# Three mixtures in one launch: remainders, sums and row transposes moved in the instruction order of an attention and two expert layers

## The chip, the cores and the metric

The kernel runs on one core of a Trainium2 chip, as one launch. The metric is the device time of a run in microseconds (us). All work is in float32, or in pairs of rounded float32 values (below).

## The reference

The computation has three parts. The first is an attention with random features. With 4 batches, 8 heads, 576 rows and 64 columns, and 128 features `omega`, it is, cut to what matters:

```python
def phi(x):                       # x scaled by D ** -0.25
    h = x @ omega.T - sum(x * x) / 2
    return exp(h - max(h)) / sqrt(m)
kv = k_p.T @ v;  z = sum(k_p)
attn = (q_p @ kv) / (q_p @ z + 1e-06)
```

The second is a dense mixture over 2304 rows of 512 columns, with 8 experts of 1024 hidden columns. `P` is a table of 2304 x 8 weights, made of the gate's logits by 8 rounds of row and column normalization:

```python
for e in range(8):
    out += P[:, e:e+1] * (relu(x @ w1[e]) @ w2[e])
```

The third is a sparse mixture on the result. A row whose product with `w_skip` is not over 0 is passed through. Each other row goes to the one expert with its largest logit, and has `gate * (relu(x @ w1[e]) @ w2[e])` added.

## The kernel before

**Pairs.** A float32 value is split into a copy rounded for TensorE (`hi`, made on ScalarE) and the *remainder* (`lo`, value minus copy, a subtraction that mostly runs on VectorE). A product is then three matmuls: hi by hi, hi by lo, lo by hi. Each engine runs its instructions in the order in which the code issues them. Buffers are waited for: an instruction that writes a buffer waits until the last reader of its earlier content is done.

**Attention.** 36 units of work (9 of k, 9 of q, and the same for the second half) run through a pipeline, one unit entering per `step`. `stage_a` transposes a unit into a PSUM bank `pt` (L426), copies it (`xh`, L429) and makes its remainder (`xl`, L431). `stage_b` projects it into `pa` (L456), takes the maximum and makes the bias `nb` (L459 to L461). `stage_x` is the exponentials (L469). For k, `stage_ck` adds up `kvp` (L489). For q, `stage_cq` transposes the result in two groups into PSUM banks `pb` (L524) and copies them (`qpt`, L525), `stage_dq` forms the quotient (L549 to L564), and `stage_eq` transposes that for the next layer into a `pb` (L589). `pt` and all `pb` share two PSUM banks, tag "b" of the pool `ps_b`. Steps 12, 21 and 30, where k turns to q or q to k, are `turn`; those and steps 11, 20 and 29 are `quiet`. In quiet steps the code puts the subtraction for `xl` into a list `rest` and issues it behind `stage_b`.

**Dense mixture.** It goes in three passes over 768 rows each. A pass has 32 steps, 8 experts by 4. Pass 0 is written in `first` and `second`. Passes 1 and 2 are written in `fast`, which works out each product of 2 x 2 blocks from seven products of sums and differences instead of eight. Step n has seven *first products* for itself (L305, six matmuls each) and, between them, seven *second products* for step n - 1 (`prod2`, six matmuls each, L1133). From the first products come seven combinations `ct[n, 0]` to `ct[n, 6]`. VectorE adds (L1239, L1265, L1279), ScalarE applies relu, GpSimd weighs by `P` (L1199) and combines (L1203). Each combination is split by `hi_a` (L1208, ScalarE) and `lo_a` (L1211, VectorE). The order of the second products, with the combination that each reads first, is

```python
SEC = ((0, 0, (0, 0)), (1, 1, 0), (3, 3, (1, 1)), (2, 6, 2), (4, 4, (0, 1)), (6, 2, 1), (5, 5, (1, 0)))
```

So the fifth reads combination 4, the sixth combination 6 and the seventh combination 5. The second and the sixth add up in PSUM banks of their own through the whole pass. The others share banks 2 and 3, and VectorE adds each of them to a sum in SBUF at once (L1144), which frees the banks for the next of them. The order of a step on TensorE is: first products 0 and 1, second 0, first 2, second 1, first 3, second 2, first 4, second 3, first 5, second 4, first 6, seconds 5 and 6.

**Sums of a pass.** `fin_steps` combines the seven sums into the four quarters of the result (L1150 is its `add`). Behind pass 1 its parts are spread over the next steps; behind pass 2 they stand in the code that follows the loop.

**The end.** Behind the last step, its second products alternate with the first products of the sparse mixture: two slots of 128 rows of the largest expert, whose rows are known early, through `split_a` (L1319 and L1321) and `products_a` (L1345). Then `route` makes the logits of the last two groups of rows from the sums (L826), picks experts and counts them on VectorE (L837 to L854), has the counts added up on TensorE (L869 to L879), and GpSimd writes the rows' numbers into a table. `rows_of_sums` transposes the sums into rows (L804, copies L805) and sends them to memory. The remaining slots follow one after the other, their experts read from that table.

Of the kernel before, what the change touches and what calls it, by code (L numbers as in the profile page):

```python
# [9 lines left out]
F32 = mybir.dt.float32  # L10
# [4 lines left out]
OP = mybir.AluOpType  # L15
# [6 lines left out]
def attn_moe_moe_kernel(  # L22
# [15 lines left out]
    nc = tc.nc  # L38
# [5 lines left out]
    P = 128  # L44
    KD = DM // P
# [371 lines left out]
            )  # L417
        loaded[nm, half, i] = t

    st, rest = {}, []  # L420

    def stage_a(nm, half, i):
        x = loaded[nm, half, i].rearrange("p h d -> p (h d)")
        pt = ps_b.tile([P, 512], F32, tag="b", name="pt")
        for c in range(KD):
            nc.tensor.transpose(pt[:, c * P : (c + 1) * P], x[:, c * P : (c + 1) * P], ident)  # L426
        xh = t_p.tile([P, KD, P], F32R, tag="xh", name="xh")
        xl = t_p.tile([P, KD, P], F32R, tag="xl", name="xl")
        nc.scalar.copy(xh, pt)  # L429
        rest.append(  # L430
            lambda: nc.vector.tensor_tensor(xl, pt.rearrange("p (c t) -> p c t", c=KD), xh.bitcast(F32), OP.subtract)  # L431
        )
        if not quiet:
            rest.pop()()
        x2 = t_p.tile([P, H, D], F32, tag="x2", name="x2")
        nc.gpsimd.tensor_tensor(x2.rearrange("p h d -> p (h d)"), x, x, OP.mult)
        st[nm, half, i] = [xh, xl, x2]
# [216 lines left out]
    for step in range(nj + 7):  # L654
# [51 lines left out]
        if step == 1:  # L706
            heat(2)
        run(1, stage_b)
        if rest:
            rest.pop()()  # L710
        if turn:
            run(3, stage_ck, "k")
            run(1, put_v)
# [432 lines left out]
    def fin_steps(p, ys=None):  # L1146

        quarter = lambda g, f: sums(p)[:, 2 * f : 2 * f + 2, g * GW : (g + 1) * GW]
        e1, e6, e7, e5 = quarter(0, 0), quarter(0, 1), quarter(1, 0), quarter(1, 1)
        add = lambda o, x: nc.vector.tensor_tensor(o, x, o, OP.add)  # L1150

        def add_y(o, k):
            if ys:
                add(o, ys[k])
            elif k == 2:
                add(o, e4)
            else:
                for h in range(2):
                    add(o[:, h], yb[BANKS[k][h]][:, :GW])

        def end():
            for t in range(2 * GT):
                done(p, t)

        return {
            "6+1": lambda: add(e6, e1),
            "7+6": lambda: add(e7, e6),
            "6+5": lambda: add(e6, e5),
            "5+7": lambda: add(e5, e7),
            "1+0": lambda: add_y(e1, 0),  # L1170
            "6+3": lambda: add_y(e6, 1),
            "7+4": lambda: add_y(e7, 2),
            "end": end,
        }

    def fin(p, n):
# [29 lines left out]
    def hi_a(n, a):  # L1206
        ha[n, a] = h_tiles(n)
        nc.scalar.copy(ha[n, a][0], ct[n, a])  # L1208

    def lo_a(n, a):  # L1210
        nc.vector.tensor_tensor(ha[n, a][1], ct[n, a], ha[n, a][0].bitcast(F32), OP.subtract)  # L1211

    def split_a2(n, a):
        hi_a(n, a)
        lo_a(n, a)

    def fast(n, x_next):
# [3 lines left out]
        def sec(j):  # L1221
            if pf:
                prod2(n - 1, j)
            elif j < 2 * GT:
                second(n - 1, j)
# [13 lines left out]
        nc.vector.tensor_tensor(c1, pz[:, :GW], c1, OP.add)  # L1239
        if pf:  # L1240
            lo_a(n - 1, 1)
            lo_a(n - 1, 4)
        weigh(n, 0, 0)
        if pf:
            split_a2(n - 1, 6)
            hi_a(n - 1, 5)
        x_next(2)
        pump(None, "pool")
        sec(0)
        product(py, 4, 4, n, False)  # L1250
        c2 = ct[n, 1] = c_tile(1)
        nc.scalar.copy(c2, py[:, :GW])
# [34 lines left out]
        x_next(8)  # L1287
        sec(5)
        sec(6)

    def drain():
        while side:
# [28 lines left out]
            eng.tensor_tensor(lo, t, hi.bitcast(F32), OP.subtract)  # L1321
        return hi, lo

    def split_a(s, r, c, part=None):

        if not 0 < s < NE:
            eng = nc.vector
            if r:
                tag = ("raw1", "raw1", "raw2", "wsum")[c]
                if part == 1:  # L1330
                    t = wa[c, r]
                else:
                    t = w1s_p.tile([P, 2, DM], F32R, tag=tag, name="sw1", bufs=2 + (c < 2))
                    t = t[:, 0], t[:, 1]
                wa[c, r] = split(zc[c], *t, eng, part)
            else:
                t = wa[c, r] if part == 1 else [xg_p.tile([P, DM], F32R, tag=f"x{x}{c}", name="sx" + x) for x in "hl"]
                wa[c, r] = split(ebuf[1][:, c], *t, eng, part)
# [46 lines left out]
    for n, (p, e, i) in enumerate(steps):  # L1385
# [57 lines left out]
        if p:  # L1443
            if p > 1 and e == 0 and i == 0:
                fin(p - 1, n)
            fast(n, x_next)
            if i == 0 and n + KI < ns_:
                load_pw(*steps[n + KI][:2])
            fetch_w2(n + 1)
            if n == ns_ - 2 * KI:  # L1450
                e_1 = reg_at(reg0, 0, [ET.Pool], E - 1)
                w_0 = rows_of(w1b, e_1), rows_of(w2b, e_1)
                nc.gpsimd.dma_start(ebuf[1][:, :KD], w_0[0][:, :, : FF // 2])
                plan[ns_ - 1, 2] = [lambda: first_w(0, 1)]
                for pos, c, part in ((3, 0, 0), (4, 0, 1), (4, 1, 0), (5, 1, 1)):
                    plan.setdefault((ns_ - 1, pos), []).append(lambda c=c, part=part: split_a(0, 0, c, part))
                plan[ns_ - 2, 8] = [first_x]
            if n == ns_ - 1:
                first_w(2, 3)
            continue  # L1460
# [38 lines left out]
    hbs += [xg_p.tile([P, FF // 2], F32, tag=tag, name="hb") for tag in ("xh6", "xl6")]  # L1499
    do = fin_steps(NP - 1)  # L1500
    split_a2(end_, 1)
    lo_a(end_, 4)
    p1 = m_bank()
    products_a(0, p1, range(0, 2))
    split_a(0, 0, 2)
    prod2(end_, 0)
    split_a2(end_, 6)
    prod2(end_, 1)
    split_a(0, 0, 3)
    products_a(0, p1, range(2, 3))  # L1510
    prod2(end_, 2)
    split_a2(end_, 5)
    do["6+1"]()
    prod2(end_, 3)
    for c in range(KD):
        split_a(0, 1, c, 0)
    products_a(0, p1, range(3, 4))
    nc.scalar.activation(out=hbs[0], in_=p1, func=AF.Relu)
    for k in (4, 5):
        xhs.append(xg_p.tile([P, KD, P], F32R, tag=f"xh{k}", name="xhs"))  # L1520
        xls.append(xg_p.tile([P, KD, P], F32R, tag=f"xl{k}", name="xls"))
    xsplit(1)
    do["1+0"]()
    prod2(end_, 4)
    do["7+6"]()
    p1 = m_bank()
    products_a(0, p1, range(0, 2), 1)
    prod2(end_, 5)
    do["6+5"]()
    prod2(end_, 6)  # L1530
    products_a(0, p1, range(2, 4), 1)
    do["6+3"]()
    do["5+7"]()
    do["7+4"]()
    mst.close()
# [116 lines left out]
    def go(r, n=1):  # L1652
        for _ in range(n):
            next(r)

    go(ra, GT - 1)
    for c in range(2):
        split_a(0, 1, c, 1)
    hsplit(0, 0, 1)
    go(ra)  # L1660
    go(rb, GT)
    go(ra)
    go(ta, GT)
    write_out()
    split_b(0, 0, 1, 2, 3, part=0)
    for c in range(2, KD):
        split_a(0, 1, c, 1)
    go(rb)
    p1 = ps_p.tile([P, 512], F32, tag="p1", name="p1")
    products_a(1, p1, range(0, 2))  # L1670
    go(tb, GT)
    writes += last
    write_out()
    yst.close()
    ps_1 = ctx.enter_context(tc.tile_pool(name="ps_1", bufs=2, space=PSUM))
    pys = [ps_1.tile([P, 512], F32, tag=f"py{i}", name=f"py{i}", bufs=1) for i in range(2)]
    split_b(0, 0, 1, part=1)
    products_a(1, p1, range(2, 4))
    relu(1, p1)
    hsplit(1, 0, 0)  # L1680
    hsplit(0, 1, 0)
    p1 = ps_p.tile([P, 512], F32, tag="p1", name="p1")
    products_a(1, p1, range(0, 1), 1)
    hsplit(1, 0, 1)
    split_b(0, 2, 3, part=1)
    split_b(0, 4, 5, 6, 7, part=0)
# [105 lines left out]
```

## Time and profile before

| | |
|---|---|
| runs | 1778.37, 1778.49, 1782.36 us; median 1778.49 |
| profiled execution | 1779.85 us, span 1778.3 us |
| granted clock of TensorE, mean | 0.996 |
| TensorE matmul busy | 1750.8 us of the span |
| VectorE busy | 1391.4 us |
| ScalarE, GpSimd busy | 857.4 and 846.2 us |

Engines are PE (TensorE matmul), PEld (its weight loads), DVE (VectorE), ACT (ScalarE), POOL (GpSimd) and SP. L305 is line 305 of the kernel before. Times are counted from the span's start. The matmuls' ends are modelled, and one begins before the last has ended; so the distance between two starts tells more than a matmul's own time, and an idle time shown for PE is short of what a wait cost.

### The profile page before, as it was taken

How to read it: one execution, taken by the hardware profiler on the slowest of the kernel's cores; microseconds unless marked ns; L12 is line 12 of the kernel's file. 1: busy time of each engine (PE TensorE's matmuls, PEld its weight loads, DVE VectorE, ACT ScalarE, POOL GpSimd, SP SyncE). 2: the span in 40 equal slices, each digit the busy share in tenths (PEclk: the TensorE clock that was granted, in tenths of full speed). 3: DMA queues.
4: the chain of work that ended last, by engine and by line, in shares of the span. 5: the costliest groups of instructions: out<-in, count | busy, mean ns of one | idle time of the engine just before them, and what ended most of it. 6: DMA issues, size and time to landing. Idle time of an engine off the chain costs nothing. (4 is left out here: it accounts for less than half of the span.)

```text
span 1778.3 us, 29140 instructions
## 1 busy us (share of the span) xinstructions
PE 1750.8 (98%) x10181; PEld 1664.9 (94%) x10181; DVE 1391.4 (78%) x2546; ACT 857.4 (48%) x1870; POOL 846.2 (48%) x857
## 2 busy tenths in 40 slices
PE   9999999999999999999999999999999999999998
PEld 9989988888888888999999999999999999999876
DVE  7868477767776777787888888888887888787887
ACT  6858444444444444434444444454443444344476
POOL 5243044436644443554555555545554555455442
PEclk9999999999999999999999999999999999999999
DMA  8241378879998888987876768787778778787271
GB/s 212 75 141 38 123 285 282 293 285 348 331 315 308 298 323 331 343 259 254 284 251 230 287 248 312 269 315 252 257 242 278 246 263 262 270 284 248 99 258 51
DMA packets 224336, 446.81 MB, mean 251 GB/s; under 512 B 25880, under 2 KB 120184, under 8 KB 224176
## 3 DMA queue, kind: packets, MB, share of 16 engines
q1 hardware_dynamic: 220592, 437.14, 71.2%
q0 software_dynamic: 3312, 7.61, 1.2%
q8 instruction: 83, 1.36, 0.3%
q14 instruction: 77, 0.63, 0.1%
q10 hardware_dynamic: 272, 0.07, 0.0%
HBM read 323.47 MB, written 134.83 MB: 258 GB/s over the span
## 5 line engine op out<-in xcount | busy, mean ns | idle before, releaser
L305 PE MATMUL m<-xh,w1h 128*128 128x384 f32 x1330 | 446.0, 335 | 0.3 <-DVE x L1309 0.2
L305 PE MATMUL m<-xl,w1h 128*128 128x384 f32 x1330 | 445.6, 335 | 0.0
L305 PE MATMUL m<-xh,w1l 128*128 128x384 f32 x1330 | 444.6, 334 | 0.0
L1199 POOL TENSOR_TENSOR c<-c,pw 128x384 f32<-128x384 f32 x192 | 214.8, 1119 | 448.7 <-ACT c L1198 447.3
L305 PEld LDWEIGHTS m<-xh,w1h 128*128 128x128 f32 x1330 | 249.7, 188 | 9.8 <-DVE rc L776 0.9
L305 PEld LDWEIGHTS m<-xl,w1h 128*128 128x128 f32 x1330 | 249.7, 188 | 8.6
L1144 DVE TENSOR_TENSOR eb<-y,eb 128x384 f32<-128x384 f32 x496 | 251.8, 544 | 0.3
L305 PEld LDWEIGHTS m<-xh,w1l 128*128 128x128 f32 x1330 | 249.7, 188 | 0.0
L1133 PE MATMUL y<-hh,wb 128*128 128x384 f32 x768 | 196.9, 337 | 0.2 <-DVE e L1144 0.2
L1211 DVE TENSOR_TENSOR hl<-c,hh 128x384 fp32r<-128x384 f32 x192 | 150.1, 782 | 47.2 <-ACT hh L1208 47.2
L1211 DVE TENSOR_TENSOR hl<-s,hh 128x384 fp32r<-128x384 f32 x256 | 185.9, 739 | 1.4
L1198 ACT ACTIVATE c<-c 128x384 f32<-128x384 f32 x192 | 101.1, 527 | 175.3 <-DVE c L1279 82.3
L1133 PE MATMUL y<-hh,w2h 128*128 128x384 f32 x512 | 173.4, 339 | 4.3 <-DVE eb L1144 4.3
L1133 PE MATMUL y<-hl,w2h 128*128 128x384 f32 x512 | 171.4, 335 | 0.0
L1133 PE MATMUL y<-hh,w2l 128*128 128x384 f32 x512 | 171.3, 335 | 0.0
L1208 ACT CAST hh<-c 128x384 fp32r<-128x384 f32 x192 | 98.7, 514 | 121.6 <-POOL c L1199 119.1
L1037 PE MATMUL y<-w2h,hl 128*128 128x512 f32 x384 | 152.4, 397 | 0.0
L1037 PE MATMUL y<-w2l,hh 128*128 128x512 f32 x384 | 151.7, 395 | 0.0
L1037 PE MATMUL y<-w2h,hh 128*128 128x512 f32 x384 | 149.5, 389 | 0.0
L1208 ACT CAST hh<-s 128x384 fp32r<-128x384 f32 x256 | 123.1, 504 | 33.5 <-POOL s L1203 33.4
L1133 PEld LDWEIGHTS y<-hh,wb 128*128 128x128 f32 x768 | 137.6, 188 | 0.7 <-DVE e L1144 0.5
L1203 POOL TENSOR_TENSOR s<-c,c 128x384 f32<-128x384 f32 x128 | 130.5, 1020 | 5.7 <-DVE c L1271 0.9
(347 smaller groups left out, 3527.5 us busy)
## 6 DMA issues: line engine op xcount, KB each, us to landing
wb<-w2c SPq DMA_DIRECT2D x128, 384.0 KB
w1h<-w1c SPq DMA_DIRECT2D x64, 640.0 KB
w1l<-w1c SPq DMA_DIRECT2D x64, 640.0 KB
w2h<-w2c SPq DMA_DIRECT2D x64, 512.0 KB
w2l<-w2c SPq DMA_DIRECT2D x64, 512.0 KB
w2c<-eb SPq DMA_DIRECT2D x58, 512.0 KB
w1c<-w1h SPq DMA_DIRECT2D x32, 896.0 KB
w1c<-w1l SPq DMA_DIRECT2D x32, 896.0 KB
```

Source lines behind the costliest of these rows:

```text
L305: nc.tensor.matmul(ps[:, :GW], x[:, a, c, :], y[:, c, :], start=first and m == 0, stop=m == 3 * KC - 1, skip_group_check=True,)
L1037: nc.tensor.matmul(ys[t], a[:, ts], b[:, f], start=i == 0 and f == 0 and m == 0, stop=i == KI - 1 and f == 1 and m == 2,)
L1133: nc.tensor.matmul(o, x[:, h * P : (h + 1) * P], y, start=m == 0 and (own or e == i == 0), stop=m == 2 and (own or e == E - 1 and i == KI ...
L1144: nc.vector.tensor_tensor(dst[:, h], o, dst[:, h], OP.add)
L1198: nc.scalar.activation(out=t, in_=t, func=AF.Relu)
L1199: nc.gpsimd.tensor_tensor(t, t, pw[steps[n][:2]][:, g], OP.mult)
L1203: nc.gpsimd.tensor_tensor(t, ct[n, x], ct[n, y], op)
L1208: nc.scalar.copy(ha[n, a][0], ct[n, a])
L1211: nc.vector.tensor_tensor(ha[n, a][1], ct[n, a], ha[n, a][0].bitcast(F32), OP.subtract)
```

## The change

- In the attention, the list `rest` goes. The subtraction for `xl` is issued in `stage_a` right behind the copy in all steps, the quiet ones too.
- In `fast`, the remainder of combination 4 is issued at the end of its own step, behind the last second product, instead of behind the first two first products of the next step. The remainder of combination 6 is issued behind the first second product, and so behind its sums of L1144, instead of ahead of them. The rounded copies stay where they were.
- In the last step, the remainders for the first two blocks of the sparse mixture's weights go to GpSimd, and the order of copies and remainders is changed.
- Behind the last step, the sums are formed in another order: "6+1" and the new "4+6" run on GpSimd; "5+6", "6=5+3" take the place of "7+6", "6+5" and "6+3". Remainders and copies there change places with products.
- In the routing, one remainder (`hsplit(0, 0, 1)`) moves behind the first group's counts, and the row transposes of both groups alternate with single blocks of `products_a` instead of standing together. A transposition of the hidden block changes places with a product.

```diff
-    st, rest = {}, []
+    st = {}
...
-        rest.append(
-            lambda: nc.vector.tensor_tensor(xl, pt.rearrange("p (c t) -> p c t", c=KD), xh.bitcast(F32), OP.subtract)
-        )
-        if not quiet:
-            rest.pop()()
+        nc.vector.tensor_tensor(xl, pt.rearrange("p (c t) -> p c t", c=KD), xh.bitcast(F32), OP.subtract)
...
         run(1, stage_b)
-        if rest:
-            rest.pop()()
...
-        add = lambda o, x: nc.vector.tensor_tensor(o, x, o, OP.add)
+        add = lambda o, x, eng=nc.vector: eng.tensor_tensor(o, x, o, OP.add)
...
-            "6+1": lambda: add(e6, e1),
+            "6+1": lambda: add(e6, e1, nc.vector if ys else nc.gpsimd),
...
+            "5+6": lambda: add(e5, e6),
+            "4+6": lambda: add(e4, e6, nc.gpsimd),
+            "6=5+3": lambda: [
+                nc.vector.tensor_tensor(e6[:, h], yb[BANKS[1][h]][:, :GW], e5[:, h], OP.add) for h in range(2)
+            ],
...
             lo_a(n - 1, 1)
-            lo_a(n - 1, 4)
         weigh(n, 0, 0)
         if pf:
-            split_a2(n - 1, 6)
+            hi_a(n - 1, 6)
             hi_a(n - 1, 5)
         x_next(2)
         pump(None, "pool")
         sec(0)
+        if pf:
+            lo_a(n - 1, 6)
...
         sec(5)
         sec(6)
+        lo_a(n, 4)
...
-                for pos, c, part in ((3, 0, 0), (4, 0, 1), (4, 1, 0), (5, 1, 1)):
-                    plan.setdefault((ns_ - 1, pos), []).append(lambda c=c, part=part: split_a(0, 0, c, part))
+                for pos, c, part in ((3, 0, 0), (4, 1, 0), (4, 0, 1), (4, 1, 1)):
+                    plan.setdefault((ns_ - 1, pos), []).append(
+                        lambda c=c, part=part: split_a(0, 0, c, part, nc.gpsimd)
+                    )
...
     split_a2(end_, 1)
-    lo_a(end_, 4)
...
-    split_a2(end_, 6)
+    hi_a(end_, 6)
     prod2(end_, 1)
-    split_a(0, 0, 3)
+    split_a(0, 0, 3, 0)
+    do["6+1"]()
     products_a(0, p1, range(2, 3))
+    split_a(0, 0, 3, 1)
     prod2(end_, 2)
-    split_a2(end_, 5)
-    do["6+1"]()
+    hi_a(end_, 5)
+    lo_a(end_, 6)
+    products_a(0, p1, range(3, 4))
     prod2(end_, 3)
-    for c in range(KD):
-        split_a(0, 1, c, 0)
-    products_a(0, p1, range(3, 4))
...
+    do["1+0"]()
     xsplit(1)
-    do["1+0"]()
     prod2(end_, 4)
-    do["7+6"]()
+    lo_a(end_, 5)
+    for c in range(KD):
+        split_a(0, 1, c, 0)
+    do["4+6"]()
     p1 = m_bank()
     products_a(0, p1, range(0, 2), 1)
     prod2(end_, 5)
-    do["6+5"]()
+    do["5+6"]()
     prod2(end_, 6)
     products_a(0, p1, range(2, 4), 1)
-    do["6+3"]()
+    do["6=5+3"]()
     do["5+7"]()
     do["7+4"]()
...
+    go(ra)
     hsplit(0, 0, 1)
-    go(ra)
     go(rb, GT)
     go(ra)
-    go(ta, GT)
+    p1 = ps_p.tile([P, 512], F32, tag="p1", name="p1")
+    for c in range(2):
+        go(ta)
+        products_a(1, p1, range(c, c + 1))
+    go(ta)
     write_out()
...
     go(rb)
-    p1 = ps_p.tile([P, 512], F32, tag="p1", name="p1")
-    products_a(1, p1, range(0, 2))
-    go(tb, GT)
+    for c in range(2, KD):
+        go(tb)
+        products_a(1, p1, range(c, c + 1))
+    go(tb)
...
-    products_a(1, p1, range(2, 4))
     relu(1, p1)
     hsplit(1, 0, 0)
-    hsplit(0, 1, 0)
     p1 = ps_p.tile([P, 512], F32, tag="p1", name="p1")
     products_a(1, p1, range(0, 1), 1)
+    hsplit(0, 1, 0)
```

## Rows read from the trace of the kernel before

**Rows 1.** Busy time, granted clock (PEclk), DMA share and GB/s of five stretches (us).

```profile
97.00:103.00 6.00, 4.53 (x26) 4.53 (x27) 2.06 (x8) 2.88 (x10) 0.00 (x0) 0.72 0.00 1
143.00:148.00 5.00, 4.04 (x20) 3.83 (x20) 1.98 (x4) 1.97 (x6) 1.04 (x1) 0.66 0.18 52
...
210.00:640.00 430.00, 429.88 (x2143) 383.98 (x2142) 312.40 (x488) 201.27 (x390) 205.64 (x220) 1.00 0.85 302
640.00:1640.00 1000.00, 996.26 (x5719) 981.25 (x5718) 813.57 (x1485) 428.62 (x900) 516.79 (x486) 1.00 0.79 274
1640.00:1700.00 60.00, 56.54 (x332) 50.06 (x331) 49.83 (x125) 27.16 (x54) 24.97 (x30) 1.00 0.39 136
```

**Rows 2.** TensorE's waits, 40 to 160 us: total, times, longest.

```profile
PE pb L524 <- DVE xl L431: 4.2, 3, 2.0
PE pb L589 <- DVE xl L431: 2.3, 2, 1.9
PE pt L426 <- ACT qpt L525: 1.4, 2, 0.7
PE pb L524 <- ACT qpt L525: 1.3, 1, 1.3
```

**Rows 3.** TensorE's waits, 640 to 1640 us.

```profile
PE y L1133 <- DVE eb L1144: 3.7, 18, 0.2
```

**Rows 4.** TensorE's waits, 1640 to 1700 us.

```profile
PE m L1345 <- DVE sxl L1321: 0.7, 1, 0.7
PE y L1133 <- DVE eb L1144: 0.7, 1, 0.7
PE m L804 <- ACT rows L805: 0.7, 1, 0.7
...
PE y L1133 <- DVE e L1144: 0.2, 1, 0.2
```

**Rows 5.** TensorE in order of time, pass 1: start, length, idle before.

```profile
947.21 0.34 PE L305 MATMUL m<-xh,w1l 128*128 128x384 f32 x1
947.77 0.44 PE L1133 MATMUL y<-hh,w2h 128*128 128x384 f32 x1 [0.22 <-DVE eb L1144]
948.05 0.34 PE L1133 MATMUL y<-hh,w2l 128*128 128x384 f32 x1
```

**Rows 6.** VectorE in order of time, step 20 of the attention.

```profile
97.74 0.68 DVE L431 TENSOR_TENSOR xl<-pt,xh 128x512 fp32r<-128x512 f32 x1
```

**Rows 7.** TensorE in order of time, step 21 of the attention.

```profile
98.47 0.66 PE L589 MATMUL pb<-ident,x 128*128 128x128 f32 x4 [1.88 <-DVE xl L431]
```

**Rows 8.** VectorE in order of time, the step of rows 5 and its end.

```profile
944.43 1.06 DVE L1211 TENSOR_TENSOR hl<-c,hh 128x384 fp32r<-128x384 f32 x1
945.41 1.84 DVE L1211 TENSOR_TENSOR hl<-s,hh 128x384 fp32r<-128x384 f32 x2
947.17 1.01 DVE L1144 TENSOR_TENSOR eb<-y,eb 128x384 f32<-128x384 f32 x2
948.11 0.54 DVE L1211 TENSOR_TENSOR hl<-s,hh 128x384 fp32r<-128x384 f32 x1
...
956.26 1.01 DVE L1144 TENSOR_TENSOR eb<-y,eb 128x384 f32<-128x384 f32 x2
958.57 0.56 DVE L1239 TENSOR_TENSOR c<-m,c 128x384 f32<-128x384 f32 x1 [1.30 <-PE m L305]
```

**Rows 9.** ScalarE in order of time, the same step's end.

```profile
956.34 0.50 ACT L1208 CAST hh<-s 128x384 fp32r<-128x384 f32 x1
```

**Rows 10.** VectorE in order of time, behind the last step.

```profile
1662.19 1.37 DVE L1211 TENSOR_TENSOR hl<-s,hh 128x384 fp32r<-128x384 f32 x1
...
1677.13 0.96 DVE L1150 TENSOR_TENSOR eb<-e,eb 128x768 f32<-128x768 f32 x1
```

**Rows 11.** GpSimd in order of time, the last step and behind it.

```profile
1654.79 1.00 POOL L1199 TENSOR_TENSOR c<-c,pw 128x384 f32<-128x384 f32 x1 [3.51 <-ACT c L1198]
...
1660.83 1.02 POOL L1203 TENSOR_TENSOR s<-c,s 128x384 f32<-128x384 f32 x1
```

More of the change, by code (lines that the diff above doesn't have):

```diff
@@ L1322, in split, with split_a @@
         return hi, lo
-    def split_a(s, r, c, part=None):
+    def split_a(s, r, c, part=None, eng=nc.vector):
         if not 0 < s < NE:
-            eng = nc.vector
             if r:
```

## The prediction

> **What bounds the kernel now.** I read the stretches first [rows 1], then what TensorE waited for in each of three stretches [rows 2 to 4], then, at each kind of wait, the rows around it. From 210 to 640 us TensorE is busy for 429.88 of 430 us, from 640 to 1640 for 996.26 of 1000 [rows 1]. So TensorE sets the time, and only what fills its gaps, or ends a half clock, can shorten the run. Since the stretch behind the attention has no gaps, time saved in the attention is not lost there: its loads are asked for as buffers come free, and they would come earlier by the same amount.
>
> Three places have gaps that the diff touches.
>
> First, the attention's turns. Four kinds of wait hold TensorE for 4.2 + 2.3 + 1.4 + 1.3 = 9.2 us, and 6.5 of it ends with the remainder `xl` of L431 [rows 2]. In the two stretches of 6 and 5 us behind the longest of these waits the granted clock was 0.72 and 0.66 in the mean [rows 1], so part of each ran at the lower of its two levels, 1.2 GHz. That is 6 x 0.28 = 1.7 us and 5 x 0.34 = 1.7 us of lost work at most; I take 1.7 and 1.5, since the second stretch begins in the wait itself.
>
> Second, passes 1 and 2 of the first mixture of experts: the second products waited 18 times for the sums of L1144, 3.7 us by the waits [rows 3]. The rows show more: 5719 matmuls in 1000 us [rows 1] start 0.17 apart, across such a wait 0.56 apart, and the next one 0.28 behind [rows 5]. So one wait costs 0.39 + 0.11 = 0.50 where the view shows 0.22, and I take 0.48 at the mean of 3.7 / 18 = 0.21.
>
> Third, the end of the last pass and the routing behind it: 60 us with 56.54 busy [rows 1], with waits for a remainder of L1321, for the sums and for row copies, 0.7 each, and 0.2 for sums of L1144 into `e4` [rows 4].
>
> **The change, part by part.**
>
> *Turns.* Before, in steps 11, 12, 20, 21, 29 and 30 the subtraction that makes `xl` is issued on VectorE behind the next stage's maximum. Until then it holds one of the two PSUM banks of tag "b". In step 20 it began at 97.74 [rows 6], and TensorE's next transposes into a bank of that tag began at 98.47, after 1.88 idle [rows 7]; the transposes of steps 12 and 30 waited up to 2.0 in the same way [rows 2]. No work is added or removed: 0.68 us [rows 6] moves ahead.
> Steps 20 to 22: with the bank back early, the second group of transposes needn't wait for the first one's copy (1.3), nor the next two groups for `xl` (2.3) [rows 2]. That is 3.6, and with 1.7 of clock, if it stays up, 5.3; I take 5.2.
> Steps 12 and 30: 2.0 and 0.7 each [rows 2], 2.7. Not all is kept: the stage behind these transposes needs a `pa` buffer that the exponentials free, I reckon 0.2 later, and the earlier `xl` of 0.68 now stands ahead of the reductions, so that a later bank comes some 0.4 late (both estimates). With some 0.1 for rounding I take 2.0 each, and 1.5 of clock for the second. The work behind the moved subtraction on VectorE is late by its 0.68 at most, while that engine idled longer than this in each turn, waiting for TensorE.
> Sum of the turns: 2.0 + 5.2 + 3.5 = 10.7. Ends: 9.2 + 3.2 = 12.4 above; below, 5, if half of the waits move to the next bank or copy (first rival).
>
> *Fourth and sixth combination.* A step's first own sums of L1144 free the banks that its third second product needs. In the row shown they ran from 947.17, behind three remainders of 1.06, 1.84 (two) [rows 8], and TensorE wanted the bank at 947.21 + 0.17 = 947.38. The change takes two of the three away: sums at 944.43 + 1.06 = 945.49, the first ready by 946.03, 1.35 ahead of need. All 18 waits should go: 18 x 0.48 = 8.6.
> The sixth's remainder runs behind these sums; its reader, the sixth second product, comes some 7 us later. The fourth's goes to the step's end: VectorE finishes the last sums at 956.26 + 1.01 = 957.27 and idles 1.30 until the addition of L1239 [rows 8]. Its rounded copy is ready at 956.34 + 0.50 = 956.84 [rows 9]. Alone it takes 0.54, beside GpSimd up to 1.37 [rows 8, 10], so it ends at 958.64 at worst, and that addition is 0.07 late against a reserve of 1.35. Behind it wait the addition, the first remainder and the sums, in that order. GpSimd's weighing and combinations are held up by the same 0.5 at most; their rounded copies feed products half a step on. I cost the move at nothing; without the reserve it would be 0.07 in each of 63 steps, 4.4. Ends: 18 x 0.50 = 9.0 and nothing gained (second rival).
>
> *Last pass's end.* Two remainders of L1321 go to GpSimd in the last step, which ends the wait of 0.2 for `e4` [rows 4], worth 0.48 like those above. On GpSimd a sum of 128x384 takes 1.02 [rows 11], so I estimate 1.36 for each of these of 128x512; before the weighing that stands behind them that queue idled 3.51 [rows 11], which holds 2.7. Off VectorE's queue go one remainder (1.37 [rows 10], taken early) and two sums of 0.96 each: 3.3, so its last sum, ended at 1677.13 + 0.96 = 1678.09 [rows 10], could end at 1674.8. The two sums of 128x768 become an estimated 2.04 each on GpSimd. They are issued behind that queue's combinations and weight loads, and VectorE's "5+6" and "7+4" read what they write. Four casts of ScalarE move behind an activation and a copy; their readers, more remainders of L1321, come after VectorE's last sum. The routing's counts on VectorE, which TensorE waits for next, now also stand ahead of one remainder of 0.68.
> A GpSimd sum also blocks. A VectorE remainder with both inputs in SBUF took 0.54 alone and 1.37 beside one [rows 8, 10]. If "5+6" is held up by "4+6" for 2.0, and the sixth's remainder by "6+1" for 0.9, 0.4 of the 3.3 is left, and with the 0.6 of the remainder that the counts now precede 1.0 is won up to the counts. With free queues it is what TensorE waited ahead of them, 0.48 and twice 0.7 + 0.28, the difference of rows 5: 2.4. I take 1.2, near the blocked end.
> The Trainium skill, SBUF — State Buffer, section "Who interferes with whom", says that a VectorE instruction with two SBUF inputs and a GpSimd one that reads SBUF shut each other out for the whole instruction, whichever began first. The rows agree (0.54 against 1.37). By that rule alone this part brings 1.0 and the time is 1757.7; without it, 2.4 and 1756.3.
> Row transposes between products: the wait of 0.7 for row copies [rows 4], 1.0 with the same difference, goes, since a product of some 0.7 now stands between two tiles and covers the copy; shorter waits of the same kind should go with it. I take 1.3. The gather and the table that follow depend on TensorE's order and move along.
> Sum: 2.5. Ends: 4.5 won, where all that these 60 us are short of busy goes (3.46 [rows 1]) and 1 of restarts, and 2 lost (third rival).
>
> Total: 10.7 + 8.6 + 2.5 = 21.8. The profiled execution took 1779.85 (span 1778.3 and 1.55 around it); less 21.8 is 1758.05. The median of the runs is 1.36 below it, 1778.49, and gives 1756.7. I take **1757.5**.
>
> **Rivals.**
> 1. *The turns' waits move.* The earlier `xl` delays VectorE's reductions and so the exponentials, and TensorE waits for these or for a copy instead. For it: there are only two banks, and a third, short wait for L431 (4.2 less twice 2.0 [rows 2]) lies in a step whose order doesn't change. Against: ScalarE and VectorE had idle time in these steps. Half the turns' gain goes: 1763.
> 2. *The step's end doesn't hold the fourth's remainder.* GpSimd runs there without a break, so the remainder waits and pushes L1239 back until the sums are as late as before. It needs over 1.35 of delay, against the 0.07 worked out. Then 8.6 is missing: 1766.
> 3. *GpSimd's sums hold VectorE's chain*, so that the routing starts later than before: the two blocked stretches of 2.0 and 0.9, each once more before a sum or remainder that follows, cost 2.9 more than the 0.4 + 0.6 left above, and the rows, which wait for the counts, win nothing: 2 lost where I count 2.5 won, 1762. For it: 1.37 against 0.54 [rows 8, 10]. Against: most of VectorE's work there has one input in PSUM, and those sums stayed at 0.5 in these rows [rows 8].
> 4. *Slower.* The fourth's rounded copy comes late in most steps, VectorE stands at its remainder, and the addition and sums behind it come too late in all 63 steps. Place: the step's end; price 0.48 x 63 = 30; it decides once the copy lands over 0.43 (its lead over 957.27) + 0.83 (what of the idle time is left) + 1.35 = 2.6 later than in [rows 9]. 1758 + 8.6 + 30 = 1796.
> 5. *The turns' gain is eaten behind them*: the loads of the middle stretch can't start earlier and TensorE waits there instead, 10.7 gone, 1768. For it: its DMA share was 0.85; against: it moved 302 GB/s without a gap on TensorE [rows 1].
>
> **How the numbers follow.** Chances: forecast 0.62, rivals in order 0.17, 0.09, 0.05, 0.03, 0.04. The forecast's own range is 1752.5 (12.4 + 9.0 + 4.5 = 25.9 off 1778.49) to 1761 (8 + 8.6 + 1). With rivals 1 and 3 the range ends at 1765 and leaves out 0.16. A difference of 0.3%, 5.3 us, is about what a measurement of this kernel can tell from none. Faster by more: forecast and rivals 1 to 3 and 5, 0.97, of which 0.02 goes to no difference, for 2, 3 and 5 together; slower 0.03.
>
> **What would show it.** Right: no wait of TensorE for L431 or L525 between 40 and 160 us, a granted clock of 1.00 there, and the stretch behind the attention beginning 9 to 12 us earlier; no waits for L1144 in passes 1 and 2, its first sums some 1.5 us behind L1239; the last product of the routing 2 to 3 us earlier than these two explain. Wrong: new waits for L469 or L525 in the turns (rival 1); L1239 released by L1211 instead of TensorE (2 and 4); sums of L1150 that take 2 us (3); TensorE waiting for weight loads after 210 us (5).

## The result, and the profile after

The changed kernel takes 1764.22 us (median of 6 runs, 1763.57 to 1765.76), the kernel before 1780.58 (6 runs beside it): ratio 0.991, 95% interval 0.9897 to 0.9923. The profiled execution took 1764.05, its span 1762.5, so 15.8 less than before where 21.8 were forecast. By the medians it is 16.4 less.

The stretches that answer to [rows 1], columns as there: the two that had run in part at 1.2 GHz at their new places, the first pass, passes 1 and 2, the end.

```profile
93.00:99.00 6.00, 6.00 (x56) 6.00 (x55) 5.17 (x14) 3.32 (x11) 0.86 (x2) 1.00 0.19 51
132.00:137.00 5.00, 4.76 (x41) 4.35 (x40) 4.86 (x11) 4.40 (x16) 1.39 (x2) 1.00 0.31 93
...
200.00:630.00 430.00, 429.98 (x2143) 383.98 (x2142) 312.78 (x486) 200.77 (x388) 206.99 (x223) 1.00 0.84 301
630.00:1630.00 1000.00, 999.07 (x5732) 983.21 (x5731) 792.18 (x1489) 431.83 (x903) 536.79 (x486) 1.00 0.80 275
1630.00:1690.00 60.00, 58.37 (x339) 51.05 (x338) 49.40 (x120) 25.75 (x53) 31.12 (x33) 1.00 0.35 117
```

TensorE's waits from 40 to 160 us, answering to [rows 2] (total, times, longest): 9.2 us have become 1.5.

```profile
PE pb L520 <- DVE xl L430: 1.0, 3, 0.5
PE pa L452 <- ACT ph L465: 0.5, 2, 0.2
```

In passes 1 and 2 the waits of [rows 3] are gone, and the matmuls' view has nothing like them in their place. But only 13 more matmuls are recorded in the 1000 us than before, and at 0.174 from start to start that is 2.3 us, not 8.6. The waits of TensorE's *weight loads* in the same stretch show why:

```profile
PEld y L1127 <- DVE hl L1210: 7.4, 21, 0.4
PEld m L305 <- DVE eb L1136: 0.5, 1, 0.5
PEld m L305 <- DMA w1l<-w1c: 0.3, 1, 0.3
```

There are 21 waits for a *remainder* (`hl`, written by `lo_a`), 18 of them in the steps that waited for sums before. A weight load runs beside the matmuls ahead of it, so such a wait shows on the matmul row as a late start alone. One of these 18 steps in order of time (start, length), first VectorE, then GpSimd, the weight loads and the matmuls:

```profile
916.66 0.54 DVE L1210 TENSOR_TENSOR hl<-s,hh 128x384 fp32r<-128x384 f32 x1
917.65 0.56 DVE L1238 TENSOR_TENSOR c<-m,c 128x384 f32<-128x384 f32 x1 [0.44 <-ACT c L1234]
918.12 1.35 DVE L1210 TENSOR_TENSOR hl<-c,hh 128x384 fp32r<-128x384 f32 x1
919.39 1.01 DVE L1138 TENSOR_TENSOR eb<-y,eb 128x384 f32<-128x384 f32 x2
```
```profile
916.76 1.32 POOL L1202 TENSOR_TENSOR s<-c,s 128x384 f32<-128x384 f32 x1
918.04 1.02 POOL L1202 TENSOR_TENSOR s<-c,c 128x384 f32<-128x384 f32 x1
```
```profile
919.52 0.19 PEld L1127 LDWEIGHTS y<-hl,w2h 128*128 128x128 f32 x1 [0.34 <-DVE hl L1210]
```
```profile
919.16 0.34 PE L1127 MATMUL y<-hh,w2l 128*128 128x384 f32 x1
919.52 0.45 PE L1127 MATMUL y<-hl,w2h 128*128 128x384 f32 x1
919.81 0.34 PE L1127 MATMUL y<-hh,w2h 128*128 128x384 f32 x1
```

Read it from the top. At 916.66 VectorE takes the fourth combination's remainder, now at the step's end. Beside it GpSimd's combination lasts 1.32; it lasted 1.02 in the trace before (first line below). So GpSimd's next combination runs from 918.04 to 919.06, and the first remainder, behind the addition at 917.65, stands beside it until 919.47: 1.35, where [rows 8] have 1.06. The second second product reads it: its third matmul starts 0.36 behind the second, and the fourth 0.29 behind that, where 0.174 is usual. That is 0.19 + 0.11 = 0.30 in each of 18 steps where a wait of 0.48 was taken away. In the trace before, that third matmul (second line) came 0.15 behind the remainder's end at 945.49:

```profile
943.07 1.02 POOL L1203 TENSOR_TENSOR s<-c,s 128x384 f32<-128x384 f32 x1
945.64 0.34 PE L1133 MATMUL y<-hl,w2h 128*128 128x384 f32 x1
```

The other three waits lie in steps 80, 82 and 85 (counted as below), where VectorE also works on the routing, and they begin in another way. VectorE in step 80:

```profile
1407.48 1.04 DVE L1210 TENSOR_TENSOR hl<-s,hh 128x384 fp32r<-128x384 f32 x1
1408.45 0.54 DVE L1238 TENSOR_TENSOR c<-m,c 128x384 f32<-128x384 f32 x1
```

The fourth's remainder takes 1.04 and the addition starts right behind it, without idle time. In the trace before, VectorE idled only 0.09 ahead of the addition in this step, where it idled 1.30 in [rows 8]. So the addition is pushed back, and the first remainder with it.

By the start of a step's first addition on VectorE (L332 in the first pass, then L1239 before and L1238 after), the profiled executions can be laid side by side. Difference to the kernel before, us (steps counted from 0 in the first pass to 95; the labels are those of the experiments below, and `e11_again` is `e11_after_again`, the changed kernel profiled once more):

```
step      before   changed  e1_turns  e2_lo6  e3_lo4  e4_lo4back  e6_behind   e11_again
0         182.65    -11.55   -11.27    +0.87   +3.16     -11.54     -11.51     -11.38
33        713.55    -11.57   -11.28    +0.82   +3.17     -11.52     -11.59     -11.47
44        883.67    -10.67   -11.11    +1.28   +3.48     -11.37     -10.65     -11.30
74       1329.75    -14.35   -11.03    -3.44   +0.14     -16.14     -19.52     -14.95
94       1631.31    -13.45   -11.04    -3.57   +1.08     -16.25     -19.64     -14.11
span     1778.3     -15.8    -11.1     -3.5    +0.9      -16.9      -20.2     -14.8
```

The changed kernel won 11.55 in the attention, gave back 0.90 at the change of passes (33 to 44), won 3.68 over the 18 waits (44 to 74), lost 0.90 in three new waits of the last pass (74 to 94) and won 2.35 behind: 15.8. Executions of one kernel differ in this table too. With the attention as before, it ended 0.87 and 3.16 later in `e2_lo6` and `e3_lo4`, and the changed kernel's second profile won 0.65 behind step 94 where the first won 2.35.

### The profile page after: what moved, and what is told of

Read it like the earlier page. It is cut to its first block, busy times and chain, and to the rows that moved or that the text cites. A ratio compares the mean times of both kernels' runs of the same rounds, so it can differ in the third digit from the quotient of the medians.

```text
span 1762.5 us, 29143 instructions
## 1 busy us (share of the span) xinstructions
PE 1747.3 (99%) x10181; PEld 1661.2 (94%) x10181; DVE 1367.9 (78%) x2542; ACT 858.5 (49%) x1870; POOL 871.5 (49%) x861
## 5 line engine op out<-in xcount | busy, mean ns | idle before, releaser
L1210 DVE TENSOR_TENSOR hl<-c,hh 128x384 fp32r<-128x384 f32 x192 | 161.2, 839 | 47.1 <-ACT hh L1207 47.1
L1210 DVE TENSOR_TENSOR hl<-s,hh 128x384 fp32r<-128x384 f32 x256 | 144.6, 584 | 0.0
L1202 POOL TENSOR_TENSOR s<-c,c 128x384 f32<-128x384 f32 x128 | 134.2, 1049 | 5.3 <-DVE c L1271 0.4
```

The lines of the kernel that those rows point to most:

```text
L1202: nc.gpsimd.tensor_tensor(t, ct[n, x], ct[n, y], op)
```

## The experiments

**The turns alone** (`e1_turns`): the kernel before with

```diff
-    st, rest = {}, []
+    st = {}
...
-        rest.append(
...
+        nc.vector.tensor_tensor(xl, pt.rearrange("p (c t) -> p c t", c=KD), xh.bitcast(F32), OP.subtract)
...
-        if rest:
-            rest.pop()()
```

> The kernel before with the turns' edit alone. Theory A (the turns delivered what the two traces show, and a transfer queue that is full at the end of the first pass takes a part back): the stretch behind the attention begins 11.5 us earlier than before, the second expert pass only some 10.6 us earlier, with one new wait of TensorE for a weight load at the change of passes; the time is 10.6 to 11 us under the kernel before. Theory B (the 0.9 us at the change of passes came from the moved remainders of the combinations, not from transfers): no new wait there, 11.5 us are kept to the end.

1769.4 (1768.18 to 1770.46), ratio 0.9939 (0.9926 to 0.9953). The attention ends 11.27 earlier; 0.17 was given back at the change of passes, and all else is as before. So the turns are worth 11, and they add up with the rest. The loss at the change of passes was 0.17 here and lay between 0 and 0.94 in the profiled executions of this study, at 0.90 and 0.17 in two of the changed kernel; so neither edit alone sets it, and neither theory holds as stated.

**The sixth's remainder alone** (`e2_lo6`), the kernel before with

```diff
-            split_a2(n - 1, 6)
+            hi_a(n - 1, 6)
...
         sec(0)
+        if pf:
+            lo_a(n - 1, 6)
```

> The kernel before with the sixth combination's remainder alone moved behind the sums; the fourth's stays behind the first's. Theory G (the fourth's remainder at a step's end holds up GpSimd's combination, whose end in turn holds up the first remainder, which the second second product waits for): neither the 18 waits for the sums nor waits for a remainder of a combination; the first remainder lasts 1.06 as before, the sums begin 0.85 us earlier; 8.5 us faster than the kernel before. Rival S (both remainders must go for the sums to be in time): half of the waits stay, 2 to 5 us faster. Rival R (the wait for the first remainder comes as soon as the sums are early, whatever the fourth does): 18 waits for the remainder of 0.30 each, 3.6 us faster.

1775.7 (1773.86 to 1778.76), ratio 0.9974 (0.9965 to 0.9983). From step 44 to 74 it won 4.72, not 8.5: rival S in size, but in another place than it or theory G had named. Weight loads in passes 1 and 2, then VectorE and TensorE in the step of [rows 8]:

```profile
PEld y L1133 <- DVE eb L1144: 4.6, 18, 0.3
```
```profile
944.53 1.06 DVE L1211 TENSOR_TENSOR hl<-c,hh 128x384 fp32r<-128x384 f32 x1
945.51 1.37 DVE L1211 TENSOR_TENSOR hl<-s,hh 128x384 fp32r<-128x384 f32 x1
946.80 1.01 DVE L1144 TENSOR_TENSOR eb<-y,eb 128x384 f32<-128x384 f32 x2
947.74 1.01 DVE L1211 TENSOR_TENSOR hl<-s,hh 128x384 fp32r<-128x384 f32 x2
948.67 0.55 DVE L1211 TENSOR_TENSOR hl<-c,hh 128x384 fp32r<-128x384 f32 x1
949.14 1.01 DVE L1144 TENSOR_TENSOR eb<-y,eb 128x384 f32<-128x384 f32 x2
```
```profile
949.50 0.34 PE L305 MATMUL m<-xh,w1l 128*128 128x384 f32 x1
949.74 0.45 PE L1133 MATMUL y<-hh,w2h 128*128 128x384 f32 x1
950.02 0.34 PE L1133 MATMUL y<-hh,w2l 128*128 128x384 f32 x1
```

The fourth's remainder at its old place stands beside GpSimd's weighing (945.25, 1.22) and takes 1.37. The first sums come in time now, but VectorE is still so late that the next ones (949.14) free their bank late: the wait has moved from the third to the fourth second product and costs 0.24 + 0.28 less twice 0.174, so 0.17 here. In the mean of the 18 steps it is 0.23, by what they win less than in `e6_behind` below, (8.87 - 4.72) / 18.

**The fourth's remainder alone** (`e3_lo4`), the kernel before with

```diff
             lo_a(n - 1, 1)
-            lo_a(n - 1, 4)
...
         sec(6)
+        lo_a(n, 4)
...
-    lo_a(end_, 4)
```

> The kernel before with the fourth combination's remainder alone moved to the step's end. Theory G: the first remainder lasts 1.35 in place of 1.06 and TensorE waits for it, 0.30 in each of the 18 steps and in three steps of the last pass; 2 to 4 us faster than the kernel before. Rival R (the first remainder is late only when both are moved): no waits for it, 8.5 us faster or, where the sixth's remainder still holds the sums, no change.

1778.49 (1776.59 to 1782.41), ratio 0.9993 (0.9984 to 1.0002): no difference that can be measured. The trace separates what the time can't. From step 44 to 74 it won 3.34, and in the last pass it lost 0.94 again; the waits are those of the changed kernel, though the sixth's remainder hadn't moved. The edit at the step's end makes them by itself, as theory G has it for the 18; the three begin with the late addition, as above:

```profile
PEld y L1133 <- DVE hl L1211: 7.2, 21, 0.4
```

**The fourth's remainder back** (`e4_lo4back`): the changed kernel with the diff above reversed.

> The changed kernel with the fourth combination's remainder back behind the first's; all else as changed. Theory G: the 18 waits of 0.30 and the three of the last pass go and none for the sums returns: 6.3 us faster than the changed kernel, 1758. Rival S (two remainders ahead of the sums make them late again): 1764 to 1768.

1763.78 (1763.01 to 1764.68): as the changed kernel. The three waits of the last pass went, 18 for the sums are there at the fourth second product as in `e2_lo6`, and 44 to 74 brought 4.77. So theory G had the cause of the 18 new waits right, but not the cure: each of the two places of the fourth's remainder costs something.

**The fourth's remainder behind the sums** (`e6_behind`): the changed kernel with

```diff
         sec(0)
         if pf:
+            lo_a(n - 1, 4)
             lo_a(n - 1, 6)
...
         sec(6)
-        lo_a(n, 4)
+        if n == ns_ - 1:
+            lo_a(n, 4)
```

> The changed kernel with the fourth combination's remainder behind the first own sums, just ahead of the sixth's (in the last step at its end as changed). Theory G: with one remainder ahead of the sums and nothing at the step's end neither kind of wait is left: the first remainder lasts 1.06, the sums begin by 1.8 behind the first addition, 18 x 0.30 + 0.9 = 6.3 us faster than the changed kernel, 1758; the stretch from the second pass to the last step 8.5 us shorter than in the kernel before. Rival L (two remainders behind the first sums make the next sums late): new waits at the fourth second product, up to 0.5 in each of 63 steps, 1764 or slower.

1759.41 (1758.95 to 1759.67), ratio 0.9874 (0.9859 to 0.989), 4.8 under the changed kernel. No weight load waited for sums or for a remainder in passes 1 and 2. GpSimd, then VectorE, in the step shown above:

```profile
915.95 1.02 POOL L1202 TENSOR_TENSOR s<-c,s 128x384 f32<-128x384 f32 x1
```
```profile
917.30 1.06 DVE L1210 TENSOR_TENSOR hl<-c,hh 128x384 fp32r<-128x384 f32 x1
918.29 1.01 DVE L1138 TENSOR_TENSOR eb<-y,eb 128x384 f32<-128x384 f32 x2
919.22 1.48 DVE L1210 TENSOR_TENSOR hl<-s,hh 128x384 fp32r<-128x384 f32 x3
```

Combination 1.02, first remainder 1.06, sums 1.46 behind the addition at 916.83. From 44 to 74 it won 8.87: 18 x 0.49.

**One input in place of two at the step's end** (`e5_onein`): the changed kernel with

```diff
-        lo_a(n, 4)
+        nc.vector.tensor_copy(ha[n, 4][1], ct[n, 4])
```

> The changed kernel with the fourth combination's remainder at the step's end replaced by a plain copy of that combination into the same buffer (one input in SBUF in place of two; the product gets that copy in place of the remainder). Theory G (it is the two-input form that holds up GpSimd): GpSimd's combination beside it lasts 1.02 in place of 1.32, the first remainder 1.06 in place of 1.35, and the 18 waits of 0.30 and the three of the last pass go: 5 to 6 us faster than the changed kernel, about 1758.5. Rival P (any VectorE instruction in that place delays what follows): combination 1.32, remainder 1.35, 1764.

Its whole time, 1836.6, says nothing: the other values send other rows to other experts, and all the excess lies behind the loop; the first addition of step 94 starts 17.54 earlier than in the kernel before. In the loop, VectorE and then GpSimd:

```profile
916.59 0.34 DVE L1290 CAST hl<-s 128x384 fp32r<-128x384 f32 x1
918.04 1.16 DVE L1210 TENSOR_TENSOR hl<-c,hh 128x384 fp32r<-128x384 f32 x1
```
```profile
916.68 1.12 POOL L1202 TENSOR_TENSOR s<-c,s 128x384 f32<-128x384 f32 x1
```

The combination is 0.10 longer than alone and the first remainder 1.16, between the two theories' figures. But the copy is also shorter (0.34 against 0.54), so the run doesn't tell the number of inputs from the duration. It does show that the chain grows with how long GpSimd is held: combination, first remainder and gain from 44 to 74 are 1.02, 1.06 and 8.87 in `e6_behind`, 1.12, 1.16 and 7.29 here, 1.32, 1.35 and 3.68 in the changed kernel.

**The end alone** (`e8_tail`): the kernel before with the diffs of the last step, the sums and the routing.

> The kernel before with the edits of the last step, of the sums behind it and of the routing alone; turns as before, the fourth's and sixth's remainders as before up to the last step. Theory (as in the two traces): everything up to the last step as before, from there to the start of the routing's products 0.9 us less, from there to the last product 1.5 less, 2.3 in all, so about 1778. Rival (the gain of the end hung on the earlier remainders of the loop): under 1 us.

1783.18 (1780.94 to 1785.37), ratio 1.0011 (1.0002 to 1.002): no gain. From the last step's first addition to its last first product it took 13.60 instead of 10.44. VectorE, GpSimd and the longest wait of TensorE there:

```profile
1650.66 3.30 DVE L1216 TENSOR_TENSOR hl<-c,hh 128x384 fp32r<-128x384 f32 x1
```
```profile
1650.99 2.55 POOL L1328 TENSOR_TENSOR sxl<-eb,sxh 128x512 fp32r<-128x512 f32 x2
```
```profile
PE y L1133 <- DVE eb L1144: 1.8, 1, 1.8
```

A remainder of 0.54 took 3.30 beside the two that the edit gives to GpSimd, though by the profile it began 0.33 ahead of them, and the sums behind it were late. In the changed kernel this remainder ran earlier, ahead of GpSimd's two, and that stretch took 9.55. So the end's edit pays only together with the loop's.

**A sum back on VectorE** (`e7_sum46`): the kernel of `e6_behind` with

```diff
-            "4+6": lambda: add(e4, e6, nc.gpsimd),
+            "4+6": lambda: add(e4, e6),
```

> The kernel of the run before this one with the sum '4+6' behind the last step on VectorE in place of GpSimd. Theory: '5+6' ran 2.61 beside '4+6' in the changed kernel and would run 0.95; with 0.96 for '4+6' in VectorE's own queue the sums end 0.7 earlier, and so does TensorE's wait of 1.05 ahead of the routing: 0.4 to 0.7 us faster than that kernel. Rival: what VectorE does in its queue costs as much as the block, no change.

1757.97 (1757.93 to 1759.4), ratio 0.987 (0.9855 to 0.9885), 1.4 under `e6_behind`, and the fastest of the study together with a variant below. The spans differ by 1.7, of which 0.8 lies between the last first product and the logits, where the edit is, and another 0.8 at the change of passes, where executions of one kernel differ. VectorE's "5+6" beside GpSimd's "4+6" in the changed kernel:

```profile
1657.45 2.61 DVE L1144 TENSOR_TENSOR eb<-eb 128x768 f32<-128x768 f32 x1
```
```profile
1657.20 2.04 POOL L1144 TENSOR_TENSOR e<-eb,e 128x768 f32<-128x768 f32 x1 [3.94 <-DVE eb L1138]
```

And both on VectorE:

```profile
1650.62 0.94 DVE L1144 TENSOR_TENSOR e<-eb,e 128x768 f32<-128x768 f32 x1
1651.49 0.95 DVE L1144 TENSOR_TENSOR eb<-eb 128x768 f32<-128x768 f32 x1
```

From the last first product to the logits it took 17.40, `e6_behind` 18.20, the changed kernel 18.21, the kernel before 18.58.

**"6+1" on VectorE too** (`e12_sum61`): the kernel of `e7_sum46` with `"6+1": lambda: add(e6, e1)`.

> The fastest kernel so far with '6+1' on VectorE as well, so that GpSimd has none of the sums. Theory (a GpSimd sum costs more by what it holds up than it saves): one remainder there lasts 0.54 in place of 1.27, against 0.95 of sum in VectorE's queue; no change within 0.5 us. Rival: the queue is the limit there, and the time rises by 0.9.

1759.0 (1758.63 to 1759.89), some 1 slower than `e7_sum46`, with runs that overlap; that stretch took 17.80, 0.4 longer. By that stretch this sum is better on GpSimd.

**Rows without alternation** (`e9_rows` from the changed kernel, `e10_sum46_rows` from `e7_sum46`), and **the changed kernel again** (`e11_after_again`). The edit of the first two:

```diff
-    p1 = ps_p.tile([P, 512], F32, tag="p1", name="p1")
-    for c in range(2):
-        go(ta)
-        products_a(1, p1, range(c, c + 1))
-    go(ta)
+    go(ta, GT)
...
-    for c in range(2, KD):
-        go(tb)
-        products_a(1, p1, range(c, c + 1))
-    go(tb)
+    p1 = ps_p.tile([P, 512], F32, tag="p1", name="p1")
+    products_a(1, p1, range(0, 2))
+    go(tb, GT)
...
+    products_a(1, p1, range(2, 4))
```

> The changed kernel with the row transposes of both groups standing together again, as before; all else as changed. Theory (a product between two tiles covers the row copy): the stretch from the logits to the last product of the routing takes 17.4 as in the kernel before in place of 16.0, the wait of 0.9 for row copies is back, 1.4 us slower than the changed kernel. Rival (the gain came from the earlier counts): 16.0 to 16.3 here too, no change.

> The fastest kernel so far (fourth's remainder behind the sums, '4+6' on VectorE) with the row transposes standing together as before. In that kernel the routing took 17.5 though its transposes alternate with products, with a wait of 1.9 that the profile puts down to nothing. Theory: that wait comes with the alternation, when ScalarE's row copies lag behind; without alternation the stretch takes 17.4, no change in time. Rival (the wait is independent of it): 18.5 to 19, 1 to 1.5 us slower.

> The changed kernel once more, unchanged. If the wait of 1.9 in the routing of the kernels derived from it is a matter of the execution, it shows here in some profile or spread of the times of 1.5 us; if it hangs on the instruction order, the routing takes 16.0 again. Time 1764.2. The loss of 0.9 at the change from the first to the second pass, where the transfers fill their queue, lies between 0 and 0.9.

1766.77 (1765.25 to 1767.77), 1757.95 (1757.2 to 1758.56) and 1765.3 (1764.87 to 1765.52): without alternation 1.5 more than the changed kernel beside it in one case, the same in the other. Of the 2.6 between the spans of `e9_rows` and `e11_after_again`, 1.5 lies in the attention, which the edit doesn't touch, and 1.1 behind the logits. Two waits of TensorE in the changed kernel's second profile weren't in its first, so they are a matter of the execution:

```profile
PE pt L1603 <- issue: 0.8, 1, 0.8
...
PE pt L1603 <- ACT hb L1594: 0.6, 1, 0.6
```

The first of them stands ahead of the products that add up the counts. From these counts VectorE works out which rows of the table to read (`rows_r`), and GpSimd reads them for the first gather. The first profile, VectorE's first reading of the counts and GpSimd's reading of the table:

```profile
1678.52 0.29 DVE L1703 TENSOR_TENSOR c<-m,th_i 1x144 f32<-1x144 f32 x1
```
```profile
1682.62 0.58 POOL L922 DMA_DIRECT2D ixs<-table  x1 [3.17 <-DVE regs L1737]
```

The second profile:

```profile
1679.71 0.30 DVE L1703 TENSOR_TENSOR c<-m,th_i 1x144 f32<-1x144 f32 x1 [0.53 <-PE p L1345]
```
```profile
1683.55 0.58 POOL L922 DMA_DIRECT2D ixs<-table  x1 [4.98 <-DVE dfe L1734]
```

GpSimd's six writes into the table take the same time in both, 7.0 from the first to the last. What differs is when VectorE reads the counts: 17.0 behind the logits in the first profile, 18.8 in the second. In the other profiles with the rows alternating it is 18.8 to 18.9, without alternation 19.4 and 17.8, in the kernel before 18.5. From the logits to TensorE's last matmul it took 93.2 in the kernel before, with the rows together, and 93.2 to 93.3 in six executions with the rows alternating; 91.7 in the first profile of the changed kernel alone. Without alternation it was 94.4 and 92.8. The alternation itself shows no gain in time. What makes the counts late in most executions stays open: the profile puts TensorE's wait ahead of them down to nothing.

## Why the prediction was right, and which step failed

The forecast was 1757.5, the result is 1764.2, inside the range that ends at 1765. That is luck in part: the forecast's own range ended at 1761, and it was widened to 1765 for rivals 1 and 3, from which the difference did not come in the main. The forecast also started from a median of 1778.49 over three runs of the kernel before; over six it is 1780.58. By the predicted steps:

**Turns, 10.7 predicted, 11.55 in the profile (11.27 alone): right.** Of these, 0.41 and 0.12 were there before step 11 of the attention, where the edit can't reach, so the turns brought 11.1 both times. By matching VectorE's and ScalarE's instructions in the two traces, 2.1 to 2.5 were won behind step 12 (2.0 predicted), 5.8 to 6.1 in steps 20 to 22 (5.2) and 2.9 to 3.2 at step 30 (3.5). No wait for L525 took the place of the old ones, though three short waits for L431 (L430 after) were left, 1.0 in all, where the prediction expected none. The clock was 1.00 in both stretches that had been at 0.72 and 0.66 [rows 1]. Of rival 1 there is a new wait for the exponentials (L469 before), 0.5, near the 0.2 for each of two turns that were reckoned.

**Fourth and sixth combination, 8.6 predicted: the step that failed.** Two of its sentences were right, the second not in all steps. A wait costs 0.48: 0.49 where both kinds went. In the 18 steps the fourth's remainder doesn't push back the addition (L1239 before): VectorE idles 0.44 ahead of it. So rival 2's mechanism isn't what happened there, though its 1766 lies near the result. What failed is the sentence that GpSimd is "held up by the same 0.5 at most; their rounded copies feed products half a step on", with the move costed at nothing. It followed what the delayed combination *feeds*, not what it *holds*: being late by 0.3, it stood beside VectorE's first remainder, and that grew from 1.06 to 1.35. Its reader, the third matmul of the second second product, had a margin of 0.15 in the trace before (remainder done at 945.49, matmul at 945.64). So 18 waits of 0.48 became 18 of 0.30. The three new ones of the last pass, 0.30 each, did come in rival 2's way, the addition pushed back, though a remainder and not the sums was late behind it. The prediction had set that aside because of an idle time of 1.30 read in one step; steps 80, 82 and 85 had 0.09. Together: 3.68 - 0.90 = 2.8.

The Trainium skill, SBUF — State Buffer, section "Who interferes with whom", says that the port pair which VectorE and GpSimd share is an exclusive lock, and that a VectorE instruction with two SBUF inputs contends with a GpSimd one that reads SBUF. The traces agree in both directions: 1.02 became 1.32 on GpSimd, 0.54 became 1.35 and 3.30 on VectorE. In the loop the prediction reckoned with one such meeting, not with the second that follows from it.

**The end, 2.5 predicted, 2.35 in that profile: the size right by luck.** One wait for sums in the last step gave 0.48, the sums 0.37, together 0.85 of 1.2. The block that the prediction expected ("5+6" held by "4+6") was there, 2.61 instead of 0.95, and undoing it brought 0.8. The rest of the gain, 1.4, is the size that the prediction gave to the row transposes (1.3), and in the first profile the counts were read 1.6 earlier behind the logits than before. But it came in one profile of seven with the alternation; in the second profile of the same kernel the whole end brought 0.65.

**The change of passes**: up to 0.9 of rival 5, not 10.7. TensorE stood for a load of `w1h` and `w1l` that was issued 10.2 earlier than before while TensorE had come 11.6 earlier. It came and went between executions: in the second profile the load was issued 12.0 earlier, and 0.17 was lost.

**Sum**: 11.55 - 0.90 + 2.8 + 2.35 = 15.8 of 21.8. The missing 6.0 is the combination term (5.8 short), the change of passes (0.9) and what the end fell short (0.15), less what the attention gave over (0.85). With the term's cause removed the kernel takes 1759.4 (`e6_behind`).

## What to carry to other kernels

When an instruction is moved beside another engine's, follow that engine's next instruction too: a delay of 0.3 us there returned to the first engine as a longer remainder and cost most of the move. Read the waits of TensorE's weight loads beside those of its matmuls, since 21 waits that took 6 us did not appear in the matmuls' view at all. A reserve read in one step doesn't hold for all: here it was 1.30 in the step shown and 0.09 in three others. And where a move pays less than its waits were worth, try a third place (here behind the sums) before undoing it.

## What the runs showed of the hardware that was not expected

The attention of the kernel before varies between executions, that of the changed kernel much less in its clock. With the turns unchanged, from 40 to 80 us the granted clock was 1.00 in two profiles and 0.96 and 0.91 in two others; first that of `e3_lo4`, then the changed kernel's, as an example of those with the turns' edit, which had 1.00 in all ten profiles:

```profile
40.00:80.00 40.00, 37.08 (x314) 35.84 (x313) 32.20 (x76) 31.62 (x96) 13.60 (x16) 0.91 0.29 80
```
```profile
40.00:80.00 40.00, 39.22 (x357) 38.04 (x356) 33.74 (x83) 33.20 (x101) 13.09 (x15) 1.00 0.28 80
```

Short waits thus cost more in some executions than in others. The 51 runs of the kernel before spread over 1777.9 to 1784.8, the 10 of the changed kernel over 1763.6 to 1765.8. In the six of each that ran side by side it was 4.0 against 2.2. So the spread was narrower with the gaps filled; that the clock alone makes it isn't shown.
